# A fused adaLN block (spectral filter and SwiGLU): x1 kept in natural column order, modulation weights read without stride, new orders of work

## The chip, the cores and the metric

The kernel runs on one core of a Trainium2 chip. The core has a matrix engine (TensorE, PE in the profile; its weight loads are listed apart as PEld), a vector engine (VectorE, DVE), a scalar engine (ScalarE, ACT), a general engine (GpSimd, POOL), and a sync engine (SyncE, SP) which here issues nearly all DMAs. The metric is device time of one execution in microseconds (us). Compared are medians of several runs.

## The reference

Input x is 2048 x 640 in bf16, c a row of 640. With one matrix product the row gives six modulation rows of 640:

```
sa, ca, ga, sb, cb, gb = split(silu(c) @ w_mod, 6)
h = layernorm(x) * (1 + ca) + sa
x = x + ga * irfft2(rfft2(h) * (w_r + 1j*w_i))        # over both axes
h = layernorm(x) * (1 + cb) + sb
x = x + gb * ((silu(h @ w_gate) * (h @ w_up)) @ w_down) # 1728 hidden columns
```

The result of the first sum is called x1 below, `h` after the second layer norm h2.

## The kernel before

The rows lie as 16 tiles of 128 (tile t holds rows 16p + t). The Fourier transforms are products with constant tables. The 640 columns are split as d = r + 5a, r from 0 to 4 and a from 0 to 127, so that a column transform is five products of 128.

Four stretches follow one another.

1. First pass. For each tile: T turns the five column sets of x (`turn`), h copies them from PSUM to SBUF, G makes the sums of the layer norm, d, p, r turn them into a scale, s scales the row table (on GpSimd, tile 14 on VectorE), B is the transform along the columns, Z its copy, S the first step along the rows (`s1`), A its copy. Ahead of it stand the products that give ca, from weights that come in two loads (`lca0`, `lca1`), and the table R scaled by it. Near its end the sa part is made (`ms`, `sacs`, `mh`, `sh`) and the filter weights are turned (J, Je, N).
2. Second pass, 17 units u: the blocks of A are turned, units 0, 1 and 16 by TensorE (T, t in this plan), the others by DMA (B, Bl); X is the rest of the row transform, Xe its copy; R and P multiply by the filter; Y turns back, y copies; E is the first inverse step, e its copy; m mirrors columns. The ga row is made here (`ga`, `gt`, `gs`) and multiplied into the table of the last inverse step (`Ri`). Loads for later go out here (L1: cb weights, L2: sb weights, L3: table H, L4: up weights).
3. Inverse pass for 16 tiles, mixed with the first FFN products: s (`s1inv`), V its copy, d (`dinv`), x (`x1_sum`: x1 = x + PSUM, with the row sum), n, q, rt, xn the second layer norm, T and f the turned and modulated h2. sb, cb and mb are the modulation products; w folds gb into the down weights; g, z, m are gate and up products, silu, product.
4. The FFN, in four groups of four tiles; the down product adds x1 and writes the output (`x_out`). The last half tile is done in two quarters, with x1 added by an identity matmul.

Everything that decides the order in the first three stretches is written out by hand: a string `plan` of step names, run from left to right. Each engine, and SP's DMA queue, executes its own instructions in the order in which the plan names them, and waits at each for what it needs. The set `ON_DVE` says which copies go to VectorE; the others go to ScalarE. PSUM is a ring: three slots in the first pass, four afterwards, and the strings `SLOTS1` and `SLOTS2` say which slot the next user takes. `T_RING` lists the tiles whose T takes a slot of the ring; the others share one fixed bank.

A modulation product (`mod_cols`, L238) is 25 pairs of weight load and matmul of 64 columns. In the kernel before, most of them load every fifth column, so that the result comes out by r:

```
lhsT=w[:, k, D * i + q:D * (i + 1):NR] if strided else w[:, k, D * i + 128 * q: D * i + 128 * (q + 1)],
```

Accordingly x1 is kept by r (columns in the order r, a), and the gate and up weights are read with rows in the order (dp c5). `x1_sum` (L723) reads x at a step of five, and `x_out` (L927) and the identity matmul (L919) read x1 at a step of 128 to get the natural order back.

## Time and profile before

| what | value |
|---|---|
| median of three runs | 266.39 us (265.93 to 267.53) |
| the profiled execution, device time | 268.39 us |
| its span, first to last instruction | 266.4 us |
| TensorE busy | 256.7 us, 96% of the span |
| VectorE, ScalarE, GpSimd busy | 148.5, 118.7, 27.2 us |
| TensorE clock granted | 1.00 throughout |

The page gives the busy time of each engine and the chain that ended last. The first pass ends near 36 us, the second near 67, the inverse pass merges with the FFN from 85 us on. A busy TensorE is not TensorE at its peak: the ends of matmuls are modelled, and matmuls overlap, so that the mean of one can be much longer than the time from one to the next.

### The profile page before, as it was taken

How to read it: one execution, taken by the hardware profiler on the slowest of the kernel's cores; microseconds unless marked ns; L12 is line 12 of the kernel's file. 1: busy time of each engine (PE TensorE's matmuls, PEld its weight loads, DVE VectorE, ACT ScalarE, POOL GpSimd, SP SyncE). 2: the span in 40 equal slices, each digit the busy share in tenths (PEclk: the TensorE clock that was granted, in tenths of full speed). 3: DMA queues.
4: the chain of work that ended last, by engine and by line, in shares of the span. 5: the costliest groups of instructions: out<-in, count | busy, mean ns of one | idle time of the engine just before them, and what ended most of it. 6: DMA issues, size and time to landing. Idle time of an engine off the chain costs nothing.

```text
span 266.4 us, 5360 instructions
## 1 busy us (share of the span) xinstructions
PE 256.7 (96%) x2208; PEld 164.6 (62%) x2212; DVE 148.5 (56%) x336; ACT 118.7 (45%) x217; POOL 27.2 (10%) x57
## 2 busy tenths in 40 slices
PE   5799989999989999999999999999999999999995
PEld 4788857988988544466644447654445664444664
DVE  4499999898499765773333352534344442333142
ACT  5389587989898686330122223022222203222000
POOL 4178920000001010200000000000000000000000
PEclk9999999999999999999999999999999999999999
DMA  7999379999697000050100013110005021000011
GB/s 239 348 341 300 90 170 184 202 350 326 189 373 255 14 25 12 0 101 25 66 20 10 0 32 69 50 59 12 0 0 98 2 74 34 12 0 0 2 49 49
DMA packets 36798, 27.88 MB, mean 105 GB/s; under 512 B 19493, under 2 KB 34214, under 8 KB 36646
## 3 DMA queue, kind: packets, MB, share of 16 engines
q1 hardware_dynamic: 36762, 27.54, 36.2%
q8 instruction: 17, 0.28, 0.5%
q14 instruction: 7, 0.06, 0.1%
q10 hardware_dynamic: 12, 0.00, 0.0%
HBM read 20.13 MB, written 2.62 MB: 85 GB/s over the span
## 4 chain that ended last, share of the span: by engine, by line
PE 87%; DMA 4%; DVE 4%; ACT 2%; SPq 1%; issue 1%; ACTq 0%
PE gu L800 41%; PE oa L922 21%; DMA first_w<-in_w_mod_dram 2%; PE yps L573 2%; PE va L708 2%; DVE late L724 2%; DMA B_all<-A_sb 2%; PE gps L308 2%; PE gu L787 2%; PE aps L353 2%; PE z L340 1%; PE aps L354 1%; PE t1ps L301 1%; PE xps L521 1%; PE oab L721 1%; PE oa L909 1%
## 5 line engine op out<-in xcount | busy, mean ns | idle before, releaser
L809 DVE TENSOR_TENSOR AT<-gu,sg 128x512 bf16<-128x512 f32 x52 | 35.8, 691 | 61.1 <-ACT sg L805 61.1
L800 PE MATMUL gu<-h2T_all,Wg 128*128 128x512 bf16 x259 | 64.4, 379 | 0.1
L800 PE MATMUL gu<-h2T_all,Wu 128*128 128x512 bf16 x257 | 64.0, 379 | 0.1
L805 ACT ACTIVATE sg<-gu 128x512 f32<-128x512 f32 x52 | 30.9, 595 | 69.4 <-PE gu L800 67.8
L922 PE MATMUL oa<-late,AT 128*128 128x320 bf16 x403 | 56.1, 299 | 0.1
L922 PEld LDWEIGHTS <-AT 128*128 128x128 bf16 x429 | 40.8, 98 | 17.2 <-issue 1.4
L800 PEld LDWEIGHTS <-Wu 128*128 128x128 bf16 x260 | 25.4, 98 | 30.7
L800 PEld LDWEIGHTS <-Wg 128*128 128x128 bf16 x260 | 25.3, 98 | 30.0
L936 DVE TENSOR_TENSOR xo<-oa,late 128x320 bf16<-128x320 f32 x31 | 20.0, 696 | 30.0 <-PE oa L909 16.8
L789 ACT ACTIVATE sg<-gu 64x512 f32<-64x512 f32 x4 | 2.4, 591 | 35.6 <-PE gu L787 35.6
L724 DVE SCALAR_TENSOR_TENSOR late<-oab,x_sb 128x640 bf16<-128x640 f32 x16 | 14.1, 901 | 4.2 <-PE oab L721 4.0
L333 POOL TENSOR_SCALAR Gs<-Gtab,rstd 128x256 bf16<-128x256 bf16 x15 | 14.0, 932 | 11.2 <-DVE rstd L323 9.8
L345 DVE SCALAR_TENSOR_TENSOR Z<-rtile,vm,z 128x640 bf16<-128x640 f32 x16 | 13.9, 872 | 0.2
L732 ACT ACTIVATE junk<-late,mean 128x640 bf16<-128x640 bf16 x16 | 13.2, 828 | 0.9 <-DVE mean L728 0.7
L708 PE MATMUL va<-Htab,Ep 128*128 128x128 bf16 x160 | 10.6, 219 | 0.8 <-DVE late L724 0.4
L367 ACT CAST A_sb<-aps 128x650 bf16<-128x650 f32 x14 | 9.9, 708 | 2.9 <-PE aps L354 2.8
L304 ACT COPY early<-t1ps 128x640 bf16<-128x640 bf16 x12 | 8.3, 695 | 5.7 <-PE t1ps L301 5.4
L715 ACT CAST VT<-va 128x640 bf16<-128x640 f32 x16 | 10.2, 701 | 0.8 <-PE va L708 0.8
L708 PEld LDWEIGHTS <-Ep 128*128 128x128 bf16 x160 | 9.7, 118 | 1.2 <-issue 0.7
L538 ACT CAST X<-xps 128x640 bf16<-128x640 f32 x14 | 9.1, 697 | 2.5 <-PE xps L529 2.4
L573 PE MATMUL yps<-identb,PP 128*128 128x128 bf16 x130 | 9.8, 220 | 0.0
L353 PE MATMUL aps<-Z,Gs 128*128 128x325 bf16 x32 | 9.3, 302 | 0.2 <-ACT Wq L442 0.2
(286 smaller groups left out, 315.2 us busy)
## 6 DMA issues: line engine op xcount, KB each, us to landing
x_sb<-in_A_x_dram SPq DMA_DIRECT2D x8, 320.0 KB, 3.4
out_dram<-xo SPq DMA_DIRECT2D x15, 160.0 KB, 1.8
Wu<-in_B_w_up_dram SPq DMA_DIRECT2D x1, 2080.0 KB
late<-in_B_w_down_dram SPq DMA_DIRECT2D x1, 2080.0 KB
wm_g<-in_w_mod_dram SPq DMA_DIRECT2D x2, 800.0 KB
Wb<-in_A_w_r_dram SPq DMA_DIRECT2D x1, 1284.0 KB
Wb<-in_A_w_i_dram SPq DMA_DIRECT2D x1, 1284.0 KB, 13.9
Wg<-in_B_w_gate_dram SPq DMA_DIRECT2D x1, 1280.0 KB
```

What stands on the lines that cost most here:

```text
L333: e.tensor_scalar(Gss[t][:, 0:2], Gtab[:, t], rstd1[:, t:t + 1], None, ALU.mult)
L345: nc.vector.scalar_tensor_tensor(Zs[t][:].rearrange("p r q -> p (r q)"), rv, vm[:, t, 1:2], held.pop(("z", t))[:, 0:D], ALU.mult, ALU.add)
L353: nc.tensor.matmul(o, lhsT=Gs[:, a, :], rhs=Z[:, :, 0:NL], start=True, stop=False)
L573: nc.tensor.matmul(yf[:, 128 * j:128 * j + 128], lhsT=PP[:, cp, 0:128] if u == 16 else PP[:, cp, 0:128, j], rhs=identb[:], start=(cp == 0) ...
L708: nc.tensor.matmul(vf[:, 128 * r:128 * r + 128], lhsT=Ep[:, t, 65 - 65 * g:193 - 65 * g, r], rhs=Htab[:, t, g, :], start=(f == 1 and r in ...
L724: nc.vector.scalar_tensor_tensor(x1[:, t, :].rearrange("p (r a) -> p r a", r=NR), VTs.pop(t).rearrange("p (r a) -> p r a", r=NR), 1.0, x_s ...
L732: nc.scalar.activation(junk[:], x1[:, t, :], ACT.Square, scale=-1.0 / D ** 0.5, bias=mean2[:, t, 1:2], accum_out=sq2[:, t:t + 1])
L800: nc.tensor.matmul(o, lhsT=w_[:, c5, fc * 128:(fc + 1) * 128], rhs=h2T(sc, c5), start=(c5 == 0), stop=(c5 == NC5 - 1))
L805: nc.scalar.activation(gus[fc][1][:], gus[fc][0][:, 0, :], ACT.Silu)
L809: nc.vector.tensor_tensor(AT[:, fc, :], gu[:, 1, :], sg[:], ALU.mult)
L922: nc.tensor.matmul(o, lhsT=AT[:, fc, tl * 128:(tl + 1) * 128], rhs=Wd_sb[:, fc, h * 320 + d0:h * 320 + d0 + n], start=(fc == 0 and not ear ...
L936: nc.vector.tensor_tensor(xos[tl][:, h * 320:(h + 1) * 320].rearrange("p (a r) -> p a r", r=NR), ps[0][0].rearrange("p (a r) -> p a r", r= ...
```

## The change

- x1 is kept in the natural column order. `x1_sum` writes it so: it reads PSUM at a step of 128 elements, x and x1 in sequence. `x_out` and the identity matmul read it in sequence. The gate and up weights are loaded with rows in the order (c5 dp).
- All calls of `mod_cols` read the weights in sequence; the parameter `strided` is gone. The ca and sa products (`ca_part`, `mod_sa`) still read with a step of five. `sacs` holds its columns so that `mod_sahat` loads weights in sequence; for that `sa_cs` is five instructions, and the constant table has its part transposed. `rinv_gate` reads the ga row at a step of five.
- In the head one x load, not two, is issued ahead of the ca weights, and the table R between the two ca loads; the other x loads and the table G alternate.
- T of tiles 1 to 7 takes ring slots, where it was tiles 1 and 3.
- All three plans, both slot strings and the set of copies on VectorE are new. Among the moves: the load of the silu table goes from the end of the second plan to the end of the first (`wm`), `ga` stands behind T1 and t1 ahead of X0, three of the four J products stand ahead of the last S, cb goes from the start of the third plan to behind d8, and with it the loads of the gate and down weights; mb goes ahead of cb; H is loaded before the up weights and the cb weights behind the sb weights.

```diff
-    T["K"] = np.concatenate([K, np.broadcast_to(cs.reshape(1, -1), (128, 125)), np.zeros((128, 3))], axis=1).astype(_NPBF)
+    T["K"] = np.concatenate([K, np.broadcast_to(cs.transpose(0, 2, 1).reshape(1, -1), (128, 125)), np.zeros((128, 3))], axis=1).astype(_NPBF)
...
-    cs_v = Ktab[:, 4 * NI:4 * NI + 125].rearrange("p (r f) -> p r f", r=NR)
+    cs_v = Ktab[:, 4 * NI:4 * NI + 125].rearrange("p (r f m) -> p r f m", r=NR, f=NR)
...
-        "A14 Je0 Je2 Xe0 Xe11 e3 e4 e7 e10 e16 f0 f1 f2 f3 f5 f6 f7 f8 f9 g15 h0 h4 y1 y3 y9 y14 y16 "
+        "A15 Xe5 Xe9 Xe12 e2 e5 e6 e8 e12 e15 f0 f1 f2 f3 f4 f7 f8 f9 g15 h0 h3 t0 t1 y3 y5 y14 y15 y16 "
...
-    def mod_cols(ps_ap, w, i=0, strided=False):
+    def mod_cols(ps_ap, w, i=0):
...
-                    lhsT=w[:, k, D * i + q:D * (i + 1):NR] if strided else w[:, k, D * i + 128 * q: D * i + 128 * (q + 1)],
+                    lhsT=w[:, k, D * i + 128 * q:D * i + 128 * (q + 1)],
...
         def sa_cs(_):
-            nc.vector.tensor_tensor(sacs[:].rearrange("p r (g q) -> p r g q", g=4)[:, :, :, 0:25], cs_v.unsqueeze(2).to_broadcast([P, NR, 4, 25]),
-                                    cps.unsqueeze(2).unsqueeze(3).to_broadcast([P, NR, 4, 25]), ALU.mult)
+            for r in range(NR):
+                nc.vector.tensor_scalar(sacs[:, r].rearrange("p (f g q) -> p f g q", f=NR, g=4)[:, :, :, 0:NR],
+                                        cs_v[:, r].unsqueeze(2).to_broadcast([P, NR, 4, NR]), cps[:, r:r + 1], None, ALU.mult)
...
-            sv = sacs[:].rearrange("p r (m f) -> p r f m", f=5)
+            sv = sacs[:].rearrange("p r (f m) -> p r f m", f=NR)
...
-        S_DVE, S_ACT, T_RING = (14,), (), (1, 3)
+        S_DVE, S_ACT, T_RING = (14,), (), (1, 2, 3, 4, 5, 6, 7)
...
-            "lx0 lx2 T0 T1 lca0 h0 G0 d0 lca1 ca lR cb T2 lx6 h1 h2 rs lx4 G1 lg2 d1 T3 lg0 T4 rvp h3 h4 p0 lg10 B0 lx8 r0 G2 d2 T5 "
+            "lx0 T0 lca0 h0 T1 lR G0 lca1 d0 lx2 lg0 lx4 ca h1 cb rs G1 T2 h2 T3 lg2 d1 B1 rvp p0 h3 G2 r0 d2 rv T5 T4 h5 lx6 G3 "
...
-            "r12 s12 Z10 ms1 B14 G15 sacs lf4 S10 A11 B15 d15 Z14 s13 mh A10 p14 S12 J1 r14 A12 Z15 s15 s14 lf7 lf5 S13 N1 Je1 S14 "
-            "A13 S15 sh A14 J3 J2 N0 A15 J0 Je3 Je2 Je0 N2 "
+            "B13 S11 B15 d15 Z13 Z15 ms3 s12 p14 ms4 s13 S10 A11 B14 S12 r14 ms1 lf6 A10 Z14 J1 s15 S13 sacs A12 J2 Je1 A13 mh Je2 "
+            "s14 N0 lf7 S14 J3 N1 A14 S15 sh J0 Je3 A15 Je0 N2 wm "
...
-            nc.vector.tensor_tensor(rf, rf, g_bc[0][:], ALU.mult)
+            nc.vector.tensor_tensor(Rinv_sb[:], Rinv_sb[:], g_bc[0][:].rearrange("p (a r) -> p r a", r=NR), ALU.mult)
...
-                nc.sync.dma_start(Wu[:], B_w_up[:, 0:FFM].rearrange("(dp c5) f -> dp c5 f", dp=P))
+                nc.sync.dma_start(Wu[:], B_w_up[:, 0:FFM].rearrange("(c5 dp) f -> dp c5 f", dp=P))
...
-            "lga T0 B4 t0 B2 T1 Bl2 Bl8 t1 X0 Xe1 Xe0 X2 lRi B6 Xe3 R1 X4 Xe2 Xe5 R0 P0 Xe4 P1 ga Y0 P2 Y1 R2 P3 y0 gt lKI R3 Y2 X6 "
-            "y2 y1 P4 Xe7 B8 Y3 B12 R4 y3 B10 Xe6 E0 e0 Y4 R5 y4 X8 E1 Xe8 R6 P6 E4 E2 P5 e1 E3 Xe9 P8 e4 R8 e2 T16 B14 e3 Y6 t16 "
-            "Y8 L1 R9 Y5 L4 y6 R7 y8 y5 P7 X10 Xe10 P9 X16 Xe11 E6 Xe16 P10 R11 Y7 e6 E5 Y9 P11 y7 P16 e5 X12 E7 y9 E8 R10 Xe12 "
...
-            "R14 E11 Y14 y15 e10 e11 E16 m0 E12 E13 y14 e12 E14 e13 e16 Ri m1 E15 e14 e15 m4 m2 m3 wm "
+            "T0 T1 t0 t1 lga ga X0 B2 B4 Xe0 Bl2 B6 Xe1 R0 Bl8 X2 P0 R1 X4 Xe2 P1 P2 Xe5 Y0 B8 Xe3 Y1 P3 R3 Xe4 lKI R2 X6 y0 Y3 y1 "
+            "P4 Xe6 Y2 Xe7 R4 y3 Y4 P5 R6 R5 y2 X8 y4 Xe8 Xe9 E0 e0 B10 R8 E2 gt B12 Y5 E3 e3 e2 P8 E4 y5 L3 lRi Y8 P9 P7 e4 R7 R9 "
+            "X10 y8 E5 E1 Xe10 Xe11 e1 E8 P6 e5 Y9 e8 T16 t16 y9 P11 Y6 P10 y6 R10 X12 Xe12 Y7 R11 B14 L4 R12 Xe13 P13 y7 P12 Y10 "
+            "X14 R13 X16 y10 E7 Xe14 Xe16 E6 R14 E10 L2 P16 m0 gs e7 P14 Xe15 Y12 Y11 e10 Y13 y12 y13 Y14 P15 e6 E9 R15 y11 Y15 E11 "
+            "y14 E12 e9 m1 e11 y15 E14 e12 E13 m2 Y16 e14 E15 e13 y16 e15 L1 m3 E16 m4 Ri e16 "
...
-        nc.vector.scalar_tensor_tensor(x1[:, t, :].rearrange("p (r a) -> p r a", r=NR), VTs.pop(t).rearrange("p (r a) -> p r a", r=NR), 1.0,
-                                       x_sb[:, t, :].rearrange("p (a r) -> p r a", r=NR), ALU.mult, ALU.add, accum_out=xsum[:, t:t + 1])
+        nc.vector.scalar_tensor_tensor(x1[:, t, :].rearrange("p (a r) -> p a r", r=NR), VTs.pop(t).rearrange("p (r a) -> p a r", r=NR), 1.0,
+                                       x_sb[:, t, :].rearrange("p (a r) -> p a r", r=NR), ALU.mult, ALU.add, accum_out=xsum[:, t:t + 1])
...
-        "sb cb s0 sx V0 cx s1 s2 V1 V2 d0 s3 s7 d2 x0 V3 d1 n0 V7 x2 s4 d3 q0 x1 s5 n2 V4 s6 x3 V5 d7 n3 x7 s8 d4 n1 q2 V6 x4 "
-        "d5 d6 V8 x6 x5 s11 s9 d8 s13 q3 q1 V9 V11 s14 d9 n7 rt x8 V13 s12 V14 xn0 nb xn1 s15 xa3 x9 V12 T0 xn2 s10 f0 f1 f2 "
...
+        "sb s0 V0 s2 s1 d0 x0 sx n0 s3 V2 s7 V1 d1 d2 V3 s8 V7 d3 x1 s4 x2 q0 V8 n1 mb n2 x3 n3 V4 d8 cb x8 q1 mx d7 q2 cx d4 "
+        "s5 x7 s13 q3 s9 x4 V5 rt V13 d5 x5 xn0 s12 V9 nb xn1 s6 s11 d9 V12 V6 T0 xn2 V11 x9 s14 xa3 f0 V14 T1 d6 f1 s15 f2 f3 "
+        "f4 f5 f6 V15 x6 f7 s10 d11 f8 f9 n9 x11 g0 V10 z0 n6 mt g1 n4 m0 z1 d15 m1 d10 x15 gA x10 d12 g6 n11 x12 q11 n7 n5 d13 "
...
-                nc.sync.dma_start(Wg[:, :, f0:f1], B_w_gate[:, f0:f1].rearrange("(dp c5) f -> dp c5 f", dp=P))
+                nc.sync.dma_start(Wg[:, :, f0:f1], B_w_gate[:, f0:f1].rearrange("(c5 dp) f -> dp c5 f", dp=P))
...
-            return x1[:, 4 * sc + tl, :].rearrange("p (r a) -> p a r", r=NR)[:, 64 * h:64 * h + 64]
+            return x1[:, 4 * sc + tl, 320 * h:320 * h + 320]
...
-                nc.vector.tensor_tensor(xos[tl][:, h * 320:(h + 1) * 320].rearrange("p (a r) -> p a r", r=NR),
-                                        ps[0][0].rearrange("p (a r) -> p a r", r=NR), x_half(tl, h), ALU.add)
+                nc.vector.tensor_tensor(xos[tl][:, h * 320:(h + 1) * 320], ps[0][0], x_half(tl, h), ALU.add)
```

More of the change, by code (lines that the diff above doesn't have):

```diff
@@ L462, in adaln_block_kernel @@
                  "d": stats, "p": root, "r": recip, "s": gscale, "B": dfwd, "Z": zcopy, "S": s1, "A": acopy,
-                 "J": turn_w, "Je": copy_w, "N": negate, "ms": mod_sa, "sacs": sa_cs, "mh": mod_sahat, "sh": sa_out}
+                 "J": turn_w, "Je": copy_w, "N": negate, "ms": mod_sa, "sacs": sa_cs, "mh": mod_sahat, "sh": sa_out,
+                 "wm": lambda _: nc.scalar.activation(warm[:], eps_t[:], ACT.Silu)}
         for w in plan.split():
@@ L635, in mods @@
             m_ps = slot("m_ps")
-            mod_cols(m_ps[:, 0], w, k, True)
+            mod_cols(m_ps[:, 0], w, k)
             return m_ps[:, 0, 0:MW * NC5:MW]
@@ L643, in ga_turn @@
             gate_turn(slot("gT_ps")[0:NC5, 0, 0:64].bitcast(BF16), 0)
-        def silu_table(_):
-            nc.scalar.activation(warm[:], eps_t[:], ACT.Silu)
         def rinv_gate(_):
-            rf = Rinv_sb[:].rearrange("p r a -> p (r a)")
-            nc.vector.tensor_tensor(rf, rf, g_bc[0][:], ALU.mult)
+            nc.vector.tensor_tensor(Rinv_sb[:], Rinv_sb[:], g_bc[0][:].rearrange("p (a r) -> p r a", r=NR), ALU.mult)
         def loads(i):
@@ L674, in adaln_block_kernel @@
                  "m": lambda i: mirror(*MCOLS[i]), "ga": mods_ga, "gt": ga_turn, "gs": lambda _: gate_spread(0),
-                 "Ri": rinv_gate, "wm": silu_table}
+                 "Ri": rinv_gate}
         for w in plan.split():
@@ L845, in adaln_block_kernel @@
              "T": pair_turn, "f": pair_affine, "gA": lambda _: ffn13(0), "g": lambda f: ffn_mm(0, f), "z": ffn_silu,
[L846 removed]
+             "m": lambda f: ffn_mul(AT2[0], f), "mA": lambda _: ffn_mul13(0, AT2[0]), "N": lambda _: ln2_power(4, 8), "mb": lambda _: late_mods("mb", wm_gb), "mx": gb_out, "mt": gb_turn,
              "sb": lambda _: late_mods("sb", wm_sb), "sx": sb_out, "cb": lambda _: late_mods("cb", wm_g, 1), "cx": cb_out, "nb": ln2_bias, "w": fold}
     plan = (
[5 rows of a table removed]
[5 rows of a table added]
     )
@@ L918, in down @@
                 for o, d0, n in ps:
-                    nc.tensor.matmul(o, lhsT=identb[:], rhs=x_half(tl, h)[:, d0 // NR:(d0 + n) // NR], start=True, stop=False)
+                    nc.tensor.matmul(o, lhsT=identb[:], rhs=x_half(tl, h)[:, d0:d0 + n], start=True, stop=False)
             for fc in range(NFC - 1):
```

13 lines of the change are left out of this document (6 added, 7 removed), and 14 rows, old and new, of the table plan.

## The prediction, made blind

> **What bounds the kernel now.** I read the page first: how busy each engine is and who makes up the chain that ended last.
>
> ```profile
> PE 256.7 (96%) x2208; PEld 164.6 (62%) x2212; DVE 148.5 (56%) x336; ACT 118.7 (45%) x217; POOL 27.2 (10%) x57
> ...
> PE 87%; DMA 4%; DVE 4%; ACT 2%; SPq 1%; issue 1%; ACTq 0%
> ```
>
> TensorE is the bound of the whole, so only two things count: matmul time that goes away, and stretches in which TensorE stands. The table of windows, cut where the work changes (first pass, the turn to the second pass, second pass, inverse pass, its end mixed with the FFN, FFN), shows where those stretches are.
>
> ```profile
> 8.04:36.24 28.20, 27.60 (x373) 24.01 (x374) 25.01 (x81) 20.36 (x39) 19.61 (x30) 1.00 0.80 251
> 36.24:41.00 4.76, 4.21 (x49) 2.45 (x47) 4.55 (x6) 3.72 (x7) 0.00 (x0) 1.00 0.93 180
> 41.00:67.03 26.03, 25.64 (x419) 22.33 (x419) 22.79 (x49) 23.23 (x41) 0.00 (x0) 1.00 1.05 271
> 67.03:85.12 18.09, 17.10 (x318) 16.59 (x316) 14.45 (x41) 17.21 (x34) 1.33 (x2) 1.00 0.89 290
> ...
> 115.63:266.44 150.81, 147.92 (x869) 81.90 (x868) 56.28 (x94) 32.26 (x53) 0.00 (x0) 1.00 0.13 33
> ```
>
> The columns are length, then busy us of PE, PEld, DVE, ACT, POOL, the clock, the DMA share and GB/s. Outside the head and the tail TensorE idles 0.60 + 0.55 + 0.39 + 0.99 = 2.5 us by 85.12. Ends of matmuls are modelled, so I also count from start to start:
>
> ```profile
> 78.70 0.44 PE L721 MATMUL oab<-Rinv_sb,VT 128*128 128x128 bf16 x5
> 79.50 1.28 PE L708 MATMUL va<-Htab,Ep 128*128 128x128 bf16 x20 [0.36 <-DVE late L724]
> ```
>
> Five such matmuls take 0.28 us on the chain; here 0.80 pass, so 0.52 is lost where the view says 0.36. Counted so, the standing between 8 and 85 us is about 5 us. That is all a new order of the same work can win there; the FFN windows are dense and their instructions don't change.
>
> **The change part by part.** *The head.* The chain begins with a load:
>
> ```profile
> GB/s 239 348 341 300 90 170 184 202 350 326 189 373 255 14 25 12 0 101 25 66 20 10 0 32 69 50 59 12 0 0 98 2 74 34 12 0 0 2 49 49
> ...
> 1.64 6.36 DMA first_w<-in_w_mod_dram
> 8.04 1.53 PE ca L372 x25
> ...
> x_sb<-in_A_x_dram SPq DMA_DIRECT2D x8, 320.0 KB, 3.4
> ```
>
> Two x loads are issued ahead of the first part of the ca weights now; afterwards one. The other's 320 KB, at the 239 and 348 GB/s of the first two slices, are 1.4 to 0.9 us; the load sits where the first slice, which holds the start-up, goes over into the second, so I take the low end: ca starts **0.95** earlier. The small second part now goes behind the 160 KB table R, 0.5 us; it is needed by the last 5 of 25 matmuls, 4/5 of 1.53 = 1.2 us after the first, so that is hidden. The moved x tiles are needed after ca; they come behind the same bytes as before, at about the time ca ends. If one is late, T2 stands up to 0.5; bounds 0 to -1.4.
>
> *Weights without stride.* Rows of one line, the four modulation products of 25 matmuls each; gb is the one already read without stride:
>
> ```profile
> L241 PE MATMUL m_ps<-sc_col,wm_g x25: 204/204/224, 42.4 to 43.4; 128*128 128x64 bf16 x25
> L241 PEld LDWEIGHTS <-wm_sb x25: 118/131/131, 67.0 to 67.9; 128*128 128x128 bf16 x25
> L241 PE MATMUL mg_ps<-sc_col,wm_sb x25: 192/204/204, 67.0 to 68.0; 128*128 128x64 bf16 x25
> L241 PE MATMUL mg_ps<-sc_col,wm_g x25: 204/204/204, 68.0 to 69.0; 128*128 128x64 bf16 x25
> L241 PEld LDWEIGHTS <-wm_gb x25: 95/98/98, 83.6 to 84.4; 128*128 128x128 bf16 x25
> L241 PE MATMUL mg_ps<-sc_col,wm_gb x25: 189/192/193, 83.7 to 84.5; 128*128 128x64 bf16 x25
> ```
>
> A weight load is 131 ns at a stride of five, 98 without; the products take 1.0 against 0.8 us. Three of them: **-0.6**. The sa-hat product gets the same treatment:
>
> ```profile
> 31.83 0.35 PE L421 MATMUL t1ps<-rtile,sacs 128*128 128x64 bf16 x5
> ...
> 33.01 0.30 PE L353 MATMUL aps<-Z,Gs 128*128 128x325 bf16 x1
> ```
>
> 30 matmuls in 1.18 us, 39 ns each, against 0.8/25 = 32: **-0.2**. Its price, sa_cs in five VectorE instructions instead of one, is under 0.3 us and stands behind the last Z of the pass, beside matmuls.
>
> *The end.* The last half tile adds x1 with an identity matmul that reads x1 in its present, turned order:
>
> ```profile
> 260.81 0.70 PE L919 MATMUL ob<-late,identb 128*128 128x160 bf16 x2
> 261.34 1.98 PE L922 MATMUL ob<-late,AT 128*128 128x160 bf16 x26
> 263.25 0.31 PE L909 MATMUL ob<-late,AT 64*128 64x160 bf16 x2
> ```
>
> Two take 0.53 us where 26 of the same shape take 1.91, 0.073 each: **-0.4**, all on the path.
>
> *x1 in natural order.* VectorE writes x1 from PSUM at 901 ns and reads it again for the output:
>
> ```profile
> L724 DVE SCALAR_TENSOR_TENSOR late<-oab,x_sb 128x640 bf16<-128x640 f32 x16 | 14.1, 901 | 4.2 <-PE oab L721 4.0
> L936 DVE TENSOR_TENSOR xo<-oa,late 128x320 bf16<-128x320 f32 x31 | 20.0, 696 | 30.0 <-PE oa L909 16.8 <-PE oa L922 13.2
> L809 DVE TENSOR_TENSOR AT<-gu,sg 128x512 bf16<-128x512 f32 x52 | 35.8, 691 | 61.1 <-ACT sg L805 61.1
> L584 DVE CAST Y<-yps 128x640 bf16<-128x640 f32 x4 | 3.3, 824 | 1.6 <-PE yps L577 1.4
> L442 DVE CAST Wq<-wps 128x1024 bf16<-128x1024 f32 x2 | 2.4, 1218 | 0.2 <-PE wps L437 0.2
> L367 DVE CAST A_sb<-aps 128x650 bf16<-128x650 f32 x1 | 0.8, 833 | 0.0
> ```
>
> The two plain copies give 1.03 ns an element and 0.17 fixed. L809 fits that; L936 doesn't, it takes 1.65 ns an element with x1 at a step of 256 bytes. Without the step it should fall to about 0.5 us, worth nothing: VectorE is busy 56 of 151 us there. In exchange L724 now reads PSUM at a step of 512 bytes. No row has just that. L367 reads PSUM at 260 bytes and pays nothing (833 for 650); L936's rate would make it 0.17 + 640 x 1.65 = 1.23 us, +0.32. I take 0.90 as now, by the row that reads the same memory; both ends are kept. [...]
>
> *Moved work.* ga goes between T1 and X0, the Silu table load from the start of the inverse pass to the end of the first, cb into the inverse pass.
>
> ```profile
> 36.24 1.51 PE L437 MATMUL wps<-Wb,jrev 128*128 128x512 bf16 x6
> 37.59 0.90 PE L496 MATMUL t2ps<-identb,A_sb 128*128 128x128 bf16 x10
> 38.75 0.46 PE L521 MATMUL xps<-Ktab,B_all 128*128 128x160 bf16 x4 [0.26 <-ACT B_all L504]
> ...
> L646 ACT ACT_TABLE_LOAD x1 | 1.3, 1283 | 0.0
> ...
> 69.31 0.15 ACT L823 COPY modcols<-mg_ps 128x5 f32<-128x5 f32 x1
> ```
>
> Now X0 begins 1.16 us after T0 and 0.6 of this is waiting; ga's 0.8 covers it. But three W products now stand ahead of the last S1 and one behind it: 0.45 us of cover where there was 1.35, for a copy of 0.83 (L367), so about 0.6 is lost before T0. A wash. The table load, with its warming 1.4 us, leaves a place where TensorE lost about 0.5 waiting for the copy at 69.31; next late there is now E16 with its copy, and e15 wholly on VectorE, 0.3 to 0.7. At its new place it stands on ScalarE behind two W copies of 1.0 us and ahead of Xe0, beside T0, ga and X0; without them it would cost up to 1.4. Another wash. cb's later place lets the Wg load start some 5 us later than now, 69.21; the first use is at 85.12, 16 us later, which hides it.
>
> ```profile
> 69.21 1.24 SPq L864 DMA_DIRECT2D Wg<-in_B_w_gate_dram  x2
> 85.12 1.24 PE L800 MATMUL gu<-h2T_all,Wg 128*128 128x512 bf16 x5
> ```
>
> The seven x tiles in the ring let T run ahead of its copies; they take no instruction away. rinv_gate loses contiguous reading, 0.48 to at most 0.9 us on VectorE, while TensorE has sb and three s1inv to do before the first inverse product. **Sum**: -0.95 - 0.6 - 0.2 - 0.4 = -2.15, the standing taken as unchanged. The profiled execution, 268.39 (span 266.44), becomes 266.2; the median of the three runs lies 2.0 below it, so 266.39 becomes **264.2**.
>
> **Rivals.** *The plans also remove standing.* They were drawn up again around the new costs, and the 5 us hold 0.4 to 0.5 us waits behind copies in several places. If half goes: 261.8. For it: VectorE idles 26.03 - 22.79 = 3.2 us in the second pass. Against: where TensorE is dense nothing is left.
>
> *VectorE or a load becomes the bound of the second pass.* There VectorE gets three more copies of 640 (0.74 from start to start) and one more mirror of 0.5: 22.79 + 2.7 = 25.5 of 26.03. ScalarE loses as much. Each wait for the fuller engine is TensorE's. And the sb weights:
>
> ```profile
> 56.74 3.49 SPq L656 DMA_DIRECT2D wm_sb<-in_w_mod_dram  x1
> ...
> wm_sb<-in_w_mod_dram SPq DMA_DIRECT2D x1, 800.0 KB, 10.2
> wm_gb<-in_w_mod_dram SPq DMA_DIRECT2D x1, 800.0 KB, 5.6
> ```
>
> Issued at 56.74 and landing after 10.2, they come at 66.9, just ahead of their use at 67.0. They stay behind Wu on SP's queue, Wu waits for T16, and T16 comes some two X-Y-E rounds later in the plan (16 rounds in 25.64 us: 3 us). What shortens the way: H now goes ahead of Wu and the cb weights go behind sb, so 0.8 MB fewer lie directly before Wu. cb's own use is 7 us further on; gb's load is issued when sb's matmuls are done, goes behind cb's and takes 5.6 us by itself, and mb is now used some 6 us after sb. If sb is late, all s1inv are queued behind it. Price of these together: 2 us more standing, 266.3.
>
> *The sum for x1 gets slower than it was* (slower than before): 0.32 us for each x1_sum, on the path for some 12 of 16, because inverse products wait for their PSUM slot behind it, as at 79.50 above. +3.9: 268.1. It decides as soon as L724 exceeds about 1.08 us, where twelve of them eat the 2.15.
>
> *The head gains nothing*, the load being bound by its own latency: 265.2.
>
> **How the numbers follow.** Forecast 0.40, less standing 0.25, VectorE or sb 0.20, slower x1_sum 0.10, head 0.05. The range reaches from the first rival to just short of the third, with the bounds of the head: 261.6 to 267.6; what is left out is a full first rival with the head's 1.4, and most of the third. About 1% is what a measurement of this kernel tells from no change, 263.7 and 269.1: faster has the first rival and a quarter of the forecast with the good end of the head, 0.38; slower has the third's upper end and stalls I overlooked, 0.12; within 0.50.
>
> **What would show it.** ca starts near 7.1 us; the L241 products take 0.8 each; the identity matmuls 0.07 each; the output sum near 0.5 us. L724's successor at 0.9 or less kills the third rival, at 1.2 it makes it. TensorE's waits between T0 and the first inverse product tell the first two apart: sums under 2.5 us of idle confirm the first, a wait of sb for its load or of yps for PP the second. A late Wg at the first gate product would prove me wrong, as would a second pass longer than 26 us.

## The result, and the profile after

The changed kernel takes 264.88 us (median of 20 runs, 264.27 to 267.23); the kernel before, run 20 times beside it on the same chip, 267.94 (265.93 to 269.04). The ratio is 0.9899, with a 95% interval of 0.9878 to 0.9921: about 1% faster. The forecast was 264.2, 2.15 us under the median of three runs then known, 266.39; against the 20 runs the gain is 3.06, and between the two profiled executions 3.3 of span (266.4 to 263.1). So the time was near the forecast and the gain larger by 0.9. An execution over 1.5% longer than the fastest of its kernel is left out of the ratios below, though not out of the medians: that concerns one of eight with the old head alone and five of twelve with the old head and the wait filled, the profiled one in both cases.

The page of the changed kernel: busy time and the shares of the chain that ended last.

```profile
PE 253.9 (97%) x2208; PEld 162.1 (62%) x2212; DVE 140.6 (53%) x343; ACT 118.1 (45%) x214; POOL 26.5 (10%) x57
...
PE 88%; DMA 7%; ACT 3%; DVE 1%; issue 0%; SPq 0%; ACTq 0%
```

TensorE is still the bound, with 2.8 us less work; transfers have 7% of the chain instead of 4%. The table of windows, cut at the same places as before (head, first pass, turn to the second pass, second pass, the wait for sb, inverse pass, its mixed end, FFN), and TensorE's longest waits (total, times, longest):

```profile
0.00:6.17 6.17, 3.72 (x33) 3.07 (x34) 2.85 (x12) 3.73 (x6) 3.09 (x21) 1.00 0.69 223
6.17:34.47 28.30, 27.49 (x379) 23.14 (x379) 25.85 (x89) 22.44 (x42) 18.85 (x30) 1.00 0.87 281
34.47:40.12 5.65, 4.64 (x96) 3.42 (x95) 3.94 (x11) 4.91 (x9) 0.00 (x0) 1.00 1.31 178
40.12:63.53 23.41, 23.41 (x369) 20.51 (x365) 22.60 (x47) 20.60 (x36) 0.00 (x0) 1.00 0.96 250
63.53:65.33 1.80, 0.16 (x4) 0.01 (x1) 1.48 (x4) 0.49 (x2) 0.00 (x0) 1.00 0.84 174
65.33:81.45 16.12, 16.11 (x311) 15.64 (x312) 12.65 (x36) 14.52 (x30) 1.27 (x2) 1.00 0.75 244
...
112.62:263.10 150.48, 147.61 (x870) 81.75 (x868) 50.19 (x95) 32.26 (x53) 0.00 (x0) 1.00 0.13 34
```

```profile
PE t1ps L398 <- DMA first_w<-in_c_dram: 2.0, 1, 2.0
PE mg_ps L241 <- DMA wm_sb<-in_w_mod_dram: 1.6, 1, 1.6
PE xps L531 <- DMA B_all<-A_sb: 0.8, 1, 0.8
PE z L340 <- ACT early L304: 0.5, 1, 0.5
```

The second pass holds no idle TensorE at all (23.41 of 23.41). Behind it TensorE stands 1.64 us for the sb weights; before, there was no such wait. The groups that the change was about:

```profile
L722 DVE SCALAR_TENSOR_TENSOR late<-oab,x_sb 128x640 bf16<-128x640 f32 x16 | 12.9, 819 | 3.0 <-PE oab L719 2.9
L934 DVE TENSOR_TENSOR xo<-oa,late 128x320 bf16<-128x320 f32 x31 | 13.4, 485 | 34.6 <-PE oa L920 18.2 <-PE oa L907 16.4
L241 PE MATMUL mg_ps<-sc_col,wm_sb x25: 192/193/203, 65.3 to 66.1; 128*128 128x64 bf16 x25
L241 PEld LDWEIGHTS <-wm_sb x25: 96/98/101, 65.3 to 66.1; 128*128 128x128 bf16 x25
```

x1's sum fell from 901 to 819 ns, the output sum from 696 to 485, the sb product from 1.0 to 0.8 us (its weight loads from 131 to 98 ns). Set beside each other by the starts on TensorE, the two executions stand so:

| from ... to | before | after | difference |
|---|---|---|---|
| start to the ca products | 8.04 | 6.17 | -1.87 |
| ca to T0, the first turn of A | 29.55 | 28.30 | -1.25 |
| T0 to the end of the last E | 29.44 | 29.06 | -0.38 |
| end of the last E to sb | 0 | 1.80 | +1.80 |
| sb to the first down product | 48.60 | 47.29 | -1.31 |
| first down product to the last | 147.62 | 147.30 | -0.32 |

Both columns are single executions. Four experiments below (x1 turned, table load back, H behind sb, sb early) leave the products of the first pass as they are in the changed kernel; their T0 stands at 34.52 to 35.28, so the 34.47 here is at the early end.

### The profile page after: what moved, and what is told of

It reads as the page before. It is cut to its first block, busy times and chain, and to the rows that moved or that the text cites. A ratio compares the mean times of both kernels' runs of the same rounds, so it can differ in the third digit from the quotient of the medians.

```text
span 263.1 us, 5355 instructions
## 1 busy us (share of the span) xinstructions
PE 253.9 (97%) x2208; PEld 162.1 (62%) x2212; DVE 140.6 (53%) x343; ACT 118.1 (45%) x214; POOL 26.5 (10%) x57
## 4 chain that ended last, share of the span: by engine, by line
PE 88%; DMA 7%; ACT 3%; DVE 1%; issue 0%; SPq 0%; ACTq 0%
PE gu L798 43%; PE oa L920 21%; DMA wm_sb<-in_w_mod_dram 4%; PE va L706 3%; PE gps L308 2%; PE z L340 2%; PE yps L575 2%; PE oab L719 1%; DMA B_all<-A_sb 1%; PE aps L353 1%; PE aps L354 1%; DMA x_sb<-in_A_x_dram 1%; PE gu L785 1%; PE t1ps L301 1%; ACT Wq L443 1%; PE xps L523 1%
## 5 line engine op out<-in xcount | busy, mean ns | idle before, releaser
L934 DVE TENSOR_TENSOR xo<-oa,late 128x320 bf16<-128x320 f32 x31 | 13.4, 485 | 34.6 <-PE oa L920 18.2
L722 DVE SCALAR_TENSOR_TENSOR late<-oab,x_sb 128x640 bf16<-128x640 f32 x16 | 12.9, 819 | 3.0 <-PE oab L719 2.9
L706 PE MATMUL va<-Htab,Ep 128*128 128x128 bf16 x160 | 10.2, 219 | 0.0
L354 PE MATMUL aps<-Z,Gs 128*128 128x315 bf16 x32 | 9.2, 298 | 0.0
L540 ACT CAST X<-xps 128x640 bf16<-128x640 f32 x13 | 8.5, 698 | 0.9 <-PE xps L531 0.7
```

The source lines that it names most:

```text
L706: nc.tensor.matmul(vf[:, 128 * r:128 * r + 128], lhsT=Ep[:, t, 65 - 65 * g:193 - 65 * g, r], rhs=Htab[:, t, g, :], start=(f == 1 and r in ...
L722: nc.vector.scalar_tensor_tensor(x1[:, t, :].rearrange("p (a r) -> p a r", r=NR), VTs.pop(t).rearrange("p (r a) -> p a r", r=NR), 1.0, x_s ...
L934: nc.vector.tensor_tensor(xos[tl][:, h * 320:(h + 1) * 320], ps[0][0], x_half(tl, h), ALU.add)
```

## The experiments

Each ran five rounds beside the kernel before. The runs were made on several chips, so ratios to the kernel before on the same chip are compared, not medians; 0.1 points are 0.27 us.

| what | median, us | ratio to before | 95% interval |
|---|---|---|---|
| the changed kernel | 264.88 | 0.9899 | 0.9878 to 0.9921 |
| before, with the new head order alone | 266.95 | 0.9976 | 0.9941 to 1.001 |
| changed, with the old head order | 265.96 | 0.9936 | 0.9898 to 0.9973 |
| before, wait for ca filled with products | 266.89 | 0.9957 | 0.9929 to 0.9986 |
| changed, old head, wait filled | 268.07 | 0.9953 | 0.9913 to 0.9994 |
| changed, strides of five and of 128 back | 266.00 | 0.9929 | 0.9905 to 0.9953 |
| changed, x1's sum in the turned order | 265.48 | 0.9918 | 0.9884 to 0.9952 |
| changed, two x tiles in the ring | 266.36 | 0.9950 | 0.9932 to 0.9968 |
| changed, table load back | 264.87 | 0.9900 | 0.9880 to 0.9920 |
| changed, H behind sb | 267.56 | 1.0004 | 0.9975 to 1.0032 |
| changed, sb early | **264.03** | **0.9855** | 0.9814 to 0.9896 |
| the same, warmed sooner | 264.04 | 0.9844 | 0.9807 to 0.9882 |
| sb early, with the old head order | 266.55 | 0.9938 | 0.9905 to 0.9971 |

### The head order, alone and undone

In the plan of the first pass of the kernel before, the head as changed:

```diff
-lx0 lx2 T0 T1 lca0 h0 G0 d0 lca1 ca lR cb T2
+lx0 T0 T1 lca0 h0 G0 d0 lR lca1 ca lx2 cb T2
```

> The kernel before with the head loads alone in the new order: x tiles 2 and 3 behind the ca weights, table R between their two parts. In the trace of the change ca starts at 6.2 us instead of 8.0. Theory (the first pass is bound by TensorE, so the head's gain goes through to the end): ca near 6.2, total 1.6 to 2.0 us below the kernel before. Rival (the first pass is held by the later x and G loads, or by VectorE, and takes part of it back): ca near 6.2, total only 0.5 to 1.2 us below.

ca began at 5.97, 2.07 earlier; the first S1 product at 13.50 instead of 15.27, T0 at 35.81 instead of 37.59. The span fell by 1.6, the lower end of the theory. By the ratio, 0.9976, it is 0.6 us, the rival's range, with an interval that reaches past 1, so by the runs alone a gain isn't settled; the trace shows that part of it went into new waits for the two x tiles now behind ca (0.22 and 0.62 us).

The counterpart, in the changed kernel:

```diff
-lx0 T0 lca0 h0 T1 lR G0 lca1 d0 lx2 lg0 lx4 ca
+lx0 lx2 T0 lca0 h0 T1 G0 lca1 d0 lR lg0 lx4 ca
```

> The changed kernel with the x tile, the tables and the two parts of the ca weights asked for in the old order (x0, x2, first part, second part, R) at its head, everything behind it as changed. If the head order is worth in the changed kernel what it was worth alone in the old one, where ca began 2.07 us earlier and the first turn of A (T0) 1.8 us earlier, ca begins near 8.0 again, T0 near 36.2, and the median is 1.5 us longer, 266.4. The rival: the changed plans have slack behind ca (ca to T0 took 28.30 where it took 29.55), and the waits for x tiles behind ca fall away when ca is late, so that only 0.5 us come through, 265.4.

By the ratios it is 1.0 us up (0.37 points), between the two expectations, though the intervals of the two ratios overlap; executions lay between 263.95 and 267.92, and the profiled one was the longest. In it T0 came at 37.67: 3.2 us later than in the changed kernel, for a ca that began only 1.82 later. So 3.2 us is the far end, not the usual cost. In this execution all that the other edits had won ahead of T0 was gone with the head. The timeline of TensorE shows where. First the kernel before, then the changed one, then this experiment (start, length, instruction, in brackets the wait ahead):

```profile
8.04 1.53 PE L372 MATMUL ca<-sc_col,first_w 128*128 128x64 bf16 x25 [1.86 <-DMA first_w<-in_w_mod_dram]
9.38 0.72 PE L301 MATMUL t1ps<-identb,x_sb 128*128 128x128 bf16 x5
10.97 0.67 PE L301 MATMUL t1ps<-identb,x_sb 128*128 128x128 bf16 x5
...
12.32 0.44 PE L301 MATMUL t1ps<-identb,x_sb 128*128 128x128 bf16 x5
```

```profile
4.60 0.74 PE L301 MATMUL t<-identb,x_sb 128*128 128x128 bf16 x5
...
6.17 1.44 PE L372 MATMUL ca<-sc_col,first_w 128*128 128x64 bf16 x25
7.45 0.45 PE L308 MATMUL gps<-early 128*128 128x130 bf16 x5
7.74 0.72 PE L301 MATMUL t<-identb,x_sb 128*128 128x128 bf16 x10
```

```profile
7.99 1.53 PE L372 MATMUL ca<-sc_col,first_w 128*128 128x64 bf16 x25 [1.44 <-DMA first_w<-in_w_mod_dram]
...
9.85 1.27 PE L301 MATMUL t<-identb,x_sb 128*128 128x128 bf16 x10
...
12.93 1.08 PE L301 MATMUL t<-identb,x_sb 128*128 128x128 bf16 x10
13.85 0.45 PE L308 MATMUL gps<-early 128*128 128x130 bf16 x5
```

Ten turning matmuls take 1.27 us in one place and 0.72 in the other. Counted from start to start, matmuls of 128 columns come every 107 ns up to some moment and every 56 ns from there on: until about 11.4 us in the kernel before, 7.3 in the changed one, 13.7 here. Where TensorE stood for the ca weights, it went on at half pace for 3.4 and 5.7 us after ca began. That suggests a second price of the wait, which isn't in the prediction. The column of the granted clock doesn't show it: it is 1.00 in the head of all three.

The wait can't be all of it, for the moment also moves where TensorE doesn't stand. With the new head, and a wait for ca of 0 to 0.38, the traces have it between about 6 and 9 us. It is latest in the run with the strides put back (below), where ca began at 6.02 without a wait and ten turning matmuls behind it still took 1.22:

```profile
7.89 1.22 PE L301 MATMUL t<-identb,x_sb 128*128 128x128 bf16 x10
```

What sets the moment isn't shown by these traces.

### The wait filled with work

To tell the wait from the pace, 18 products of the identity with itself were put into the wait, into an unused part of the ca slot. No load and no other step moved.

```diff
+            for _ in range(18):
+                nc.tensor.matmul(held["ca"][:, 512:640], lhsT=identb[:], rhs=identb[:], start=True, stop=True)
```

> The kernel before with 18 more products of the identity with itself, 107 ns each, into an unused part of the ca slot of PSUM, in the 1.86 us in which TensorE waits for the ca weights; no load and no plan is touched. In the trace of before matmuls of 128 columns start every 107 ns until about 11.5 us and every 56 ns from 11.75 on; in that of the changed kernel the pace changes at 7.3. If standing for the weights is what delays the change of pace, then here ca still begins near 8.04, the 21 matmuls between 9.4 and 11.5 run at 56 ns, the first S1 product begins near 14.2 instead of 15.27 and T0 at 36.5 instead of 37.59; the median is 0.8 to 1.1 us shorter than before's. If the pace depends on the time alone or the second half of the head waits for x loads anyway, T0 stays at 37.6 and the median equal.

```profile
6.09 1.23 PE L379 MATMUL ca<-identb 128*128 128x128 bf16 x18
8.31 1.18 PE L372 MATMUL ca<-sc_col,first_w 128*128 128x64 bf16 x25 [0.99 <-DMA first_w<-in_w_mod_dram]
9.33 0.45 PE L301 MATMUL t1ps<-identb,x_sb 128*128 128x128 bf16 x5
...
10.82 0.47 PE L301 MATMUL t1ps<-identb,x_sb 128*128 128x128 bf16 x5 [0.48 <-DMA x_sb<-in_A_x_dram]
```

The pace changed inside the 18, at 6.2. ca began at 8.31, no earlier than before, and the same turning matmuls behind it took 0.45 instead of 0.72. From ca to the first S1 product it took 6.61 instead of 7.23, with a new wait for an x tile (0.48) inside. T0 came at 37.25, only 0.34 earlier where 1.1 was expected, in part because ca itself began 0.27 later. The kernel does *more* work on TensorE and is 0.4% faster (ratio 0.9957, interval below 1, 1.2 us): the pace is a cost by itself.

The same 18 products in the changed kernel with the old head:

> The changed kernel with the old head order (its pace changed at 13.7 us, ca at 7.99, T0 at 37.67 against 34.47 of the changed kernel) and the same 18 products in the wait for the ca weights. If the loss of 3.2 us at T0 is 1.8 us of waiting and 1.4 us of slow pace, the pace changes at 8 or sooner, ca still begins near 8.0, T0 at 36.2, and the median falls by about 1.2 us against the one without the products (265.96): 264.8. If the pace isn't what costs, T0 stays near 37.7.

T0 came at 36.30, 1.4 us earlier than without them, as expected. The median didn't follow (ratio 0.9953, against 0.9936 without them; 264.8 us was expected), and the executions lay between 265.38 and 270.47. In the profiled one, 270.23, TensorE waited 3.4 us for sb behind the second pass, and the granted clock (third number from the end of the row) was down behind it:

```profile
65.40:69.08 3.68, 0.23 (x4) 0.03 (x2) 1.49 (x4) 0.57 (x2) 0.00 (x0) 1.00 1.01 351
69.08:72.00 2.92, 2.92 (x44) 2.92 (x45) 0.88 (x1) 0.61 (x2) 0.00 (x0) 0.59 0.44 99
```

Over the whole execution this makes a mean clock of 0.992. Eight of the twelve executions have 0.994 or less and took 267.23 to 270.47; the four others took 265.38 to 267.71. Only one was profiled, so that the late sb is behind the other seven too isn't shown. The head was tried once more where sb isn't late (below).

### The strides put back

All four modulation products that go through `mod_cols` load every fifth column (in the kernel before gb's did not), the sa columns are read at a step of five, and the identity matmul reads x1 at a step of 128. (What comes out is for permuted columns.)

```diff
-                    lhsT=w[:, k, D * i + 128 * q:D * i + 128 * (q + 1)],
+                    lhsT=w[:, k, D * i + q:D * (i + 1):NR],
...
-        sv = sacs[:].rearrange("p r (f m) -> p r f m", f=NR)
+        sv = sacs[:].rearrange("p r (m f) -> p r f m", f=NR)
```

> The changed kernel with strided reading put back: the modulation weights at a step of five in all four products, the sa columns at a step of five, and x1 at a step of 128 in the identity matmul. The products come out for permuted columns, the amount of work is that of the changed kernel. Theory (these loads and reads are on TensorE's path): the four products 1.0 us each instead of 0.8, the sa product 1.2 instead of 0.85, the two identity matmuls 0.5 instead of 0.15; total 1.2 to 1.6 us above the changed kernel. Rival (part of them stands in waits anyway, ga beside copies, sb ahead of late copies): 0.4 to 0.9 above.

The ratio is 0.3 points or 0.8 us up, in the rival's range, and each term can be read at its place. The timeline of its end, and the group of the sb product:

```profile
259.17 0.71 PE L918 MATMUL ob<-late,identb 128*128 128x160 bf16 x2
259.70 1.98 PE L921 MATMUL ob<-late,AT 128*128 128x160 bf16 x26
```

```profile
L241 PEld LDWEIGHTS <-wm_sb x25: 118/131/139, 65.9 to 66.9; 128*128 128x128 bf16 x25
L241 PE MATMUL mg_ps<-sc_col,wm_sb x25: 204/204/225, 65.9 to 66.9; 128*128 128x64 bf16 x25
```

The identity matmuls take 0.53 from start to start again (0.14 in the changed kernel), each product 1.0 instead of 0.8, the sa-hat product 1.18 instead of 0.84 (32.06 to 33.24 against 31.50 to 32.34). These terms of the prediction are right. The step in the output sum on VectorE was not put back.

### x1's sum in the turned order

x1_sum writes by r again: PSUM is read in sequence, x at a step of five. (Columns are permuted behind it.)

```diff
-nc.vector.scalar_tensor_tensor(x1[:, t, :].rearrange("p (a r) -> p a r", r=NR), ...
+nc.vector.scalar_tensor_tensor(x1[:, t, :].rearrange("p (r a) -> p r a", r=NR), ...
-x_sb[:, t, :].rearrange("p (a r) -> p a r", r=NR), ALU.mult, ALU.add, accum_out
+x_sb[:, t, :].rearrange("p (a r) -> p r a", r=NR), ALU.mult, ALU.add, accum_out
```

> The changed kernel with x1 written in the turned order again: PSUM in sequence, x at a step of five; what follows takes the columns as if they were natural, so that the result is for permuted columns. Theory (the PSUM step of 512 bytes costs nothing, and the x step of 10 bytes is what cost 0.08 us): the sum goes from 0.82 back to 0.90 us, and because inverse products wait for VectorE only in a few places the total rises by 0 to 0.5 us. Rival (VectorE sets the pace of the inverse pass): 16 times 0.08, total 1.0 to 1.4 us above.

```profile
L722 DVE SCALAR_TENSOR_TENSOR late<-oab,x_sb 128x640 bf16<-128x640 f32 x16 | 14.0, 890 | 2.8 <-PE oab L719 2.8
```

890 ns, close to the 901 before. So it was reading x at a step of 10 bytes that cost 0.07 to 0.08 us, and reading PSUM at a step of 512 bytes cost nothing: 819 ns is no more than the plain copy of 640 in sequence, 824 in the prediction's rows. The stretch from sb to the first down product took 47.88 instead of 47.29; but traces in which only other things were changed have 47.56 to 47.61 there (below), so of 16 x 0.071 = 1.1 us on VectorE 0.3 to 0.6 was on the path. By the runs it is 0.2 points, within the intervals.

### Two x tiles in the ring instead of seven

Tiles 2, 4, 5, 6, 7 go through the one fixed bank; T5 and T8 must then be followed by their copies, and the string `SLOTS1` loses the five entries.

```diff
-        S_DVE, S_ACT, T_RING = (14,), (), (1, 2, 3, 4, 5, 6, 7)
+        S_DVE, S_ACT, T_RING = (14,), (), (1, 3)
...
-rv T5 T4 h5 lx6
+rv T5 h5 T4 lx6
...
-T8 T7 r2 Z3 G5 lg10 h8 h7
+T8 h8 T7 r2 Z3 G5 lg10 h7
```

> The changed kernel with two turned x tiles in the ring instead of seven (1 and 3, as before); tiles 2, 4, 5, 6, 7 go through the one fixed slot, and T5 and T8 are followed at once by their copies h5 and h8, since two tiles can't lie in that slot. If the ring takes waits away, T4, T6 and T7 stand for the copy of the tile before, 0.3 to 0.4 us each by the distance of T to its copy's end in the trace of the changed kernel, and T0 comes 0.9 to 1.2 us later: 265.9. If TensorE only waits elsewhere (for the x loads or Gt), as the prediction had it, nothing changes: 264.9, T0 at 34.5 to 35.3 as in the other executions.

```profile
PE t1ps L301 <- ACT early L304: 2.2, 5, 0.8
```

Five waits for the copy of the tile before, 2.2 us together, more than the expectation had; T0 at 36.61, the ratio 0.5 points up. The prediction gave the ring nothing. In the new order it is worth 1.4 us, because T there follows T closely and only the ring lets it. What it would be worth in the old order wasn't tried.

### The table load put back

The warming Silu instruction goes from the end of the first plan to the end of the second, behind e16.

> The changed kernel with the warming Silu instruction, and with it the table load of 1.3 us on ScalarE, back from the end of the first pass to the end of the second, behind e16. If the move was a wash, 264.9 within 0.3. If the inverse pass owes part of its 1.31 us to it, the copy of the sb columns on ScalarE is late behind the table again and the stretch from sb to the first FFN product grows by 0.5, with nothing back at T0 and X0, where the load is covered: 265.4. If it stands in the way at its new place, T0 to X0 (1.72) shrinks by 0.3 to 0.5 and the sum is even or better: 264.5 to 264.9.

The time is the same (ratio 0.9900). T0 to X0 took 1.72 in both; sb to the first down product 47.56 instead of 47.29. That 0.27 doesn't belong to the load: with two x tiles in the ring, and the load where the changed kernel has it, the stretch took 47.59, with sb early 47.61. 47.29 stands only in the two traces in which TensorE waited 1.5 us or more for sb (the changed kernel and the old head alone, 47.29 both). In this run it waited 0.9 there, and then 0.4 for the gb weights, which the changed kernel's trace doesn't have:

```profile
PE mg_ps L241 <- DMA wm_gb<-in_w_mod_dram: 0.4, 1, 0.4
```

The load has cover at its old place too, beside TensorE's wait for sb (0.9 us in this execution, sb at 64.88), as ScalarE's timeline shows:

```profile
64.41 1.28 ACT L673 ACT_TABLE_LOAD   x1
```

So "a wash" holds for the kernel as it is.

### Why sb is late

SP's queue in the changed kernel (start, length of the issue, transfer), its wait at Wu, and the last piece of the chain ahead of the sb product:

```profile
44.28 0.58 SPq L656 DMA_DIRECT2D Htab<-tab_H  x1
...
45.45 2.33 SPq L487 DMA_TRANSPOSE B_all<-A_sb  x1
52.85 0.39 SPq L658 DMA_DIRECT2D Wu<-in_B_w_up_dram  x1
...
54.43 1.72 SPq L654 DMA_DIRECT2D wm_sb<-in_w_mod_dram  x1
```

```profile
SPq L658 <- DMA B_all<-A_sb: 4.9, 1, 4.9
```

```profile
54.43 10.85 DMA wm_sb<-in_w_mod_dram
```

Wu (2.08 MB by the page) takes the place of A, which the last transposing load (B14) still reads; SP waits 4.9 us at Wu for it, and sb stands behind Wu. B14 was issued behind H's 1 MB. TensorE's wait differs from one execution to the next: 1.64 in the changed kernel, 0.88 in the run with the table load back. Two ways out were tried. In the first, sb and the spreading of ga (`gs`) go ahead of Wu:

```diff
-B14 L4 R12
+B14 L2 gs L4 R12
...
-R14 E10 L2 P16 m0 gs e7
+R14 E10 P16 m0 e7
```

> The changed kernel with the load of the sb weights, and the spreading of the ga row, moved ahead of the load of the up weights, into the time in which the queue waits for the last DMA transpose. In the changed kernel TensorE stands 1.6 us in front of the sb product. Theory (that load alone holds it): the wait goes, the last copies and mirrors are next late for 0.3 to 0.6, total 1.0 to 1.6 us below the changed kernel, some 4.3 below the kernel before. Rival (the copies and mirrors of the second pass would hold the first inverse step as long): under 0.5 us below the changed kernel.

sb is issued at 48.29 and no wait for it is left: TensorE goes from the last E to sb within 0.3 us. 264.03, ratio 0.9855, and the six executions lie close together (263.32 to 264.24). By the ratios this is 1.2 us under the changed kernel, as the theory had it; by the medians, 0.85. The intervals of the two ratios still overlap a little.

In the second, H goes behind sb instead:

```diff
-y5 L3 lRi
+y5 lRi
...
-R14 E10 L2 P16
+R14 E10 L2 L3 P16
```

> The changed kernel with the 1 MB load of H moved from ahead of the last transposing load (B14) to behind the sb weights. If B14 is late because it waits behind H, then it lands some 3 us earlier than 52.66, Wu and sb, which stand behind it on SP, are asked for by T16's end, near 51.5 and 53.1 instead of 52.85 and 54.43, and TensorE's wait for sb (1.64 us) falls to 0.3 or less: 264.0, if H, now last, still lands before the first inverse product at 65. If sb is late because of the bytes ahead of it (Wu 1.3 MB and the two small ones), the wait for sb stays near 1.5. If H comes too late, TensorE waits for H in sb's place, up to 3 us: 266 to 267.

```profile
64.61 0.95 PE L241 MATMUL mg_ps<-sc_col,wm_sb 128*128 128x64 bf16 x25 [0.64 <-DMA wm_sb<-in_w_mod_dram]
67.19 3.05 PE L706 MATMUL va<-Htab,Ep 128*128 128x128 bf16 x30 [1.63 <-DMA Htab<-tab_H]
```

```profile
64.61:67.19 2.58, 0.95 (x25) 0.86 (x26) 0.69 (x3) 0.00 (x0) 0.00 (x0) 1.00 0.98 300
67.19:72.00 4.81, 4.80 (x57) 4.81 (x58) 1.97 (x4) 2.60 (x5) 0.00 (x0) 0.65 0.75 257
...
67.60:71.00 3.40, 3.40 (x36) 3.40 (x34) 1.09 (x2) 2.14 (x4) 0.00 (x0) 0.50 0.90 307
```

```profile
SPq L658 <- DMA B_all<-A_sb: 2.8, 1, 2.8
SPq L658 <- PE t2ps L498: 2.7, 1, 2.7
```

SP's wait at Wu for B14 ended after 2.8 us instead of 4.9, but then came one of 2.7 for T16, which reads A as well. Wu went out at 52.08 and sb at 53.66, 0.8 sooner than in the changed kernel; sb's transfer still took 10.9 and TensorE waited 0.64. So H ahead of B14 was the smaller part of the delay, and Wu ahead of sb the larger. Now H was late as well, 1.63, and behind the two waits the granted clock fell to 0.50 for 3.4 us, a mean of 0.65 in the row above: thirty products took 3.05 us where the changed kernel needs 1.84:

```profile
66.12 1.84 PE L706 MATMUL va<-Htab,Ep 128*128 128x128 bf16 x30
```

From the first inverse product to the first gate product it took 16.95 instead of 15.33. In this trace the wait was paid for twice. Over the runs the whole gain of the change was gone (ratio 1.0004). Eight of the twelve executions have a mean clock of 0.992 or 0.993, like the profiled one, and took 267.14 to 269.80; the four at 0.999 or 1.000 took 265.96 to 266.91.

### A sooner pace, and the head once more

On top of the version with sb early: seven identity products ahead of the first wait for c, four more behind it, and the small part of the ca weights ahead of R.

```diff
+        for _ in range(7):
+            nc.tensor.matmul(Gt[:, 0:128], lhsT=identb[:], rhs=identb[:], start=True, stop=True)
...
-        for _ in range(12):
+        for _ in range(16):
```

> The changed kernel with the sb weights asked for early (264.03), with seven identity products ahead of the first wait for c (from about 1.3 us on, when the identity is ready), four more behind it, and the small part of the ca weights asked for ahead of R. If the pace changes as soon as TensorE has been kept busy long enough, it changes near 5.5 instead of 7.3, which quickens about ten matmuls by 51 ns, and the 0.3 us wait for the last ca weights goes: 263.3 to 263.7. If the ca weights bound the head whatever the pace, only the second counts or nothing: 263.7 to 264.1.

No difference (264.04, four executions). The pace changed at 5.8, but the seven had to wait for a VectorE fill of their bank until 1.78, and the longer row of products put the first x turn off to 4.51; ca began at 6.28. T0 came at 34.28, 0.85 earlier than with sb early alone, and that was gone by the end of the second pass, with a wait of 0.4 for the table KI among the new ones. Whether the earlier pace is worth anything here stays open.

Last, the version with sb early and the old head:

> The version with the sb weights asked for early (264.03, executions between 263.3 and 264.2) with the old order of the head loads. The old head alone, put back into the changed kernel, gave a T0 3.2 us later in its profiled execution but a median only 1.1 us longer, with executions between 263.95 and 267.92; there the wait for sb stood behind it and could swallow or add to it. If the head is worth the waiting for ca and the longer slow pace, about 2 to 3 us whenever the pace changes late, the median here is 266.0 to 267.0 and the executions spread, with the late sb gone, by 2 us or more, according to when the pace changes. If the 1.1 us are the head's worth and the spread was sb's, the median is 265.1 and the spread under 1.5 us.

266.55, ratio 0.9938 against 0.9855: the old head costs 0.8 points, 2.2 us, where no late load covers or confuses it, as the first of the two expectations had it. The executions spread again, from 264.28 to 267.70. The profiled one, 264.87, was among the shorter: the ca weights came after a wait of only 0.28 and ca began at 6.47, yet the pace changed only between 10.2 and 10.5 (ten turning matmuls in 1.27 us). So in the old order both the landing of the weights and the change of pace differ from one execution to the next; in the new order the traces have ca at 5.97 to 6.28, and the change of pace still moves, between about 6 and 9 us. How much of the 2.2 us is the wait and how much the pace isn't shown. This fits the spread of the kernel before, 265.93 to 269.04, and that the first three of its runs had a median 1.5 us below that of 20.

## Why the prediction was right, and where it wasn't

The terms of the sum, each against what its place in the trace or its experiment shows:

| step of the prediction | forecast | measured |
|---|---|---|
| the head: ca starts earlier | -0.95 | -1.87 |
| (none) the pace behind ca | 0 | -1.0 |
| weights without stride, three products | -0.6 | -0.6 |
| sa-hat product | -0.2 | -0.34 |
| identity matmul at the end | -0.4 | -0.39 |
| x1's sum taken as now | 0 | -0.3 to -0.6 |
| table load, "another wash" | 0 | none seen |
| "the standing taken as unchanged": sb late | 0 | +1.8, of which 0.3 came back behind it |

The right column gives -3.0 to -3.3; the spans differ by 3.3. It is an account of one pair of executions. The -1.0 is worked out from the timeline of before: some 20 matmuls between 9.4 and 11.4 us at 107 instead of 56 ns. It is an estimate; the filled wait bears out that there is such a term (0.62 with a new wait of 0.48 inside), not its size in other executions, since the change of pace moves.

**The head** was mis-sized. The working priced the 320 KB at the rate of the first slices, with ca "near 7.1"; it began at 6.17, without any wait, so the whole wait of 1.86 was gone. The bound given, -1.4, was too narrow too: in the old order ca began at 7.99 to 8.31 in four traces and at 6.47 in a fifth, so the landing of the weights varies by more than that. The step that fails is that it took the head for a transfer alone. Behind a ca that had waited TensorE also went on at half pace, and the timeline of before, which the prediction quoted only for later stretches, carries it: behind ca the same five matmuls stand at 0.72 and then at 0.44.

**Strides, sa-hat, identity** came out about as priced, each shown where the edit was put back: products of 0.8 us, and identity matmuls of 0.07. The output sum fell to 0.485 as forecast. That this is worth nothing wasn't tried alone, but the FFN gained 0.32 us in all, no more than the identity matmuls account for.

**x1's sum** was taken at 0.90 "by the row that reads the same memory" and came at 0.82. The third rival (slower than before) is dead. The prediction overlooked that the old form had a step of its own, on x, which went away. Reading PSUM out of sequence, at a step of 512 bytes, cost VectorE nothing here (819 ns). A bf16 step of five did cost: 890 against 819 ns in the sum, and 131 against 98 for a weight load.

**The ring** was said to take no instruction away, which is so, and was given no value. In the new order it holds 1.4 us of waits off. It has no row above, since the kernel before shows no such waits ahead of T0.

**The rivals.** The first named its own test: waits between T0 and the first inverse product under 2.5 us. By the windows they are 1.01 + 0 + 1.64 = 2.65, so it isn't confirmed. But the test couldn't tell: the kernel before has 31.91 - 30.65 = 1.26 us by the same view, and the version with sb early 1.02. The second pass did lose all its standing, and VectorE, busy 22.60 of 23.41, did not become its bound, for TensorE never waits there. The other half of the second rival came true: sb stood behind Wu, landed late, and everything behind it was queued, "if sb is late, all s1inv are queued behind it". Its price, 1.8, was near the 2 it named; what it left out is that the other terms would carry it. The way there differed: Wu waited for B14's reading of A, not for T16, and H ahead of Wu, which the rival counted as shortening the way, delayed B14. Wg came in time (first gate product at 81.45 without a wait), as the prediction said. The head gained, 2.2 us where sb isn't late, so the fourth is dead.

So that the time came within 0.7 us of the forecast is in part luck, twice over. The gain, 3.1 for 2.15, came near because two errors met: ahead of T0 it was 3.1 us where the sum had 1.15, and a wait of 1.8 us that stood among the rivals took most of the surplus back. And the forecast started from a median of three runs, 266.39, that lay 1.55 below that of 20; the larger gain made up 0.9 of it.

## What to carry to other kernels

Early in a kernel, price a wait of TensorE by its length and by the work behind it that may run at half pace (here 107 instead of 56 ns a matmul); look for the same group of matmuls with two different lengths in the timeline, since the clock column may not show it (here 1.00 at both paces). When a plan is drawn up again, follow each late load back along its queue: what stands ahead of it, and what that waits for; here moving one load ahead of a waiting one made the fastest version of all. Undo an edit where nothing else can cover its effect: by the ratios the old head cost 1.0 us with the late load behind it and 2.2 us without.

## What the hardware showed that was not expected

- The half pace at the start, 107 against 56 ns for each matmul of 128 columns, ended at 5.8 to 13.7 us. The two latest, 11.4 and 13.7, are the two traces in which TensorE had stood 1.4 us or more for the ca weights with nothing in the wait; but with no wait at all it was once near 9, and once past 10 behind a wait of only 0.28.
- Later in the kernel a wait of 1.64 us did no harm to the pace (changed kernel, granted clock 1.00 behind it), but 0.64 and 1.63 with a product of 0.95 between them (H behind sb), 2.3 us of standing in 3.2, were followed by a granted clock of 0.50 for 3.4 us.
- VectorE read fp32 from PSUM at a step of 512 bytes as fast as in sequence (819 ns for 640, the plain copy 824), while bf16 from SBUF cost 0.07 us more at a step of 10 bytes (890 against 819 ns), and 696 instead of 485 ns for 320 elements at a step of 256 bytes.
